# A feed-forward kernel's start: w1's first tile on ScalarE's queue, and the first contraction tile multiplied by halves of the rows

## The chip, the core and the metric

The kernel runs on one core of a Trainium2 chip. A core has a matrix engine (TensorE, PE in the profile; its weight loads are listed as PEld), a vector engine (VectorE, DVE), an activation engine (ScalarE, ACT), GpSimd (POOL) and SyncE (SP). Each has its own instruction stream; they meet through semaphores. Matrix products are written to PSUM, here 8 banks of 128 rows by 512 32-bit columns; everything else lies in SBUF, with 128 rows (partitions). SyncE and ScalarE start transfers between the device memory and SBUF, each on a queue of its own.

The metric is the device time of one execution in microseconds. Before the change its median over 3 runs is 126.36 us (126.25 to 126.38).

## What is computed

```python
B, S, D, F = 1, 2048, 640, 1728          # bf16
h = jnp.einsum("bsd,df->bsf", x, w1)     # x: (1, 2048, 640), w1: (640, 1728)
h = silu(h)                              # h * sigmoid(h)
out = jnp.einsum("bsf,fd->bsd", h, w2)   # w2: (1728, 640)
```

## The kernel before

**Tiling.** The contraction length D = 640 of the first product is cut into DT = 5 tiles of 128 ("contraction tiles", the index `dt`). F = 1728 is cut into 13 columns of 128 (`ft`) and a last one of 64. The 2048 rows of x are handled in four chunks of SCH = 512 rows (`sc`), and a chunk in four blocks of 128 rows (JB = 4). The first product is made transposed: PSUM gets h's 128 values of `ft` on its partitions and 512 rows of x along its columns, so w1's tile [128 x 128] is the loaded weight and the transposed x, `xT_sb[:, dt, rows]`, is streamed. One bank holds one (`ft`, `sc`). Sigmoid runs on ScalarE, and VectorE multiplies it with the sums (`silu`, L196); the result `hT_sb` is the weight or the streamed operand of the second product (L300 to L350), whose results go out by DMA.

**How x gets transposed.** For chunks 1 to 3, and for the last contraction tile of chunk 0, a transposing DMA brings x into `xT_sb` (L157, L237). For the first four contraction tiles of chunk 0, x is loaded as it lies into `x0_sb` (L143) and transposed by PE, 128 x 128 at a time, against an identity (`transpose_x0`, L171): four transposes write one PSUM bank, and one copy takes them from there to `xT_sb`, on VectorE for even `dt` (L180) and on ScalarE for odd `dt` (L182).

**The order of the work.** The program is a list of operations (`Plan`, L21); each goes to its engine's stream in the order in which it was added, with waits on the semaphores of what it depends on. An engine thus works strictly in the order written. PE's stream begins like this:

1. warm-up: five matmuls of 512 columns and one of 256 on constants, whose results are not used (L169);
2. the four transposes of contraction tile 0 of x, in two halves of two blocks each, with a bank and a VectorE copy for each half (L275);
3. more warm-up: one matmul of 512 columns and one of 256 (L277);
4. `column_group` for chunk 0 (L252): for each `dt`, one matmul of 512 columns into each of FA = 6 banks (`ft` 0 to 5). The first matmul of a `dt` waits for x's and w1's tile of that `dt`. After the second matmul (`ft == 1`) the transposes of the next `dt` are put in (`transpose_next`, L269);
5. `unit` for the other columns of chunk 0 (L211), then the other chunks, and then the second product.

**The loads at the start.** SyncE issues: the first half (two of four blocks) of x's tile 0 (`x0_a`, 64 KB), w1's tiles 0, 1 and 2 for the first six columns (192 KB each), then, after a wait for x's tile 0, w1's tiles 3 and 4; then the transposing DMA of x's tile 4 (after w1's tile 1 has landed) and the rest of w1 in two pieces. ScalarE issues: the second half of x's tile 0 (`x0_b`, 64 KB), x's tiles 1, 2 and 3 (128 KB each), and then loads its activation table. In the code (L151 to L154):

```python
x0_a = [load_x0("sp", "x0_a", 0, JB // 2, 0, 1), load_x0("act", "x0_b", JB // 2, JB, 0, 1)]
w1_lo = [load_w1("sp", "w1_0", 0, 1, 0, FA * P)]
x0_c = [load_x0("act", "x0_c", 0, JB, 1, 2), load_x0("act", "x0_d", 0, JB, 2, 3), ...]
w1_lo += [load_w1("sp", f"w1_{dt}", dt, dt + 1, 0, FA * P) for dt in (1, 2)]
```

The functions that the diff touches, with the profile's line numbers:

Of the kernel before, what the change touches and what calls it, by code (L numbers as in the profile page):

```python
# [20 lines left out]
class Plan:  # L21
# [9 lines left out]
    def add(self, eng, emit, deps=(), group=None):  # L31
        op = Op(eng, emit, [d for d in deps if d is not None], group)
        self.ops.append(op)
        return op
# [40 lines left out]
def bass_standalone__dense_activation_silu__prompt_kernel(  # L75
# [13 lines left out]
    P = 128  # L89
    H = P // 2  # L90
    SCH = 512
    DT = D // P
# [5 lines left out]
    JB = SCH // P  # L98
# [4 lines left out]
    with ExitStack() as es:  # L103
        def sb(name, shape, dtype):
            return es.enter_context(nc.sbuf_tensor(name, shape, dtype))

        xT_sb = sb("xT_sb", [P, DT, S], bf16)
        w1_sb = sb("w1_sb", [P, DT, F], bf16)
# [9 lines left out]
        ps = es.enter_context(nc.psum_tensor("ps", [P, NBANK, SCH], fp32))  # L118
# [6 lines left out]
        add = plan.add  # L125
        bank_free = [[] for _ in range(NBANK)]
        turn = [0]

        def take_bank():
            b = turn[0] % NBANK  # L130
            turn[0] += 1
            return b


        FA = 6
# [7 lines left out]
        def load_x0(eng, name, j0, j1, d0, d1):  # L143
            return add(eng, lambda e: e.dma_start(
                out=x0_sb[:, j0:j1, d0 * P:d1 * P], in_=x0_v[:, j0:j1, d0 * P:d1 * P]), group=name)

        def load_w1(eng, name, d0, d1, f0, f1, deps=()):
            return add(eng, lambda e: e.dma_start(
                out=w1_sb[:, d0:d1, f0:f1], in_=w1_v[:, d0:d1, f0:f1]), deps, group=name)

        x0_a = [load_x0("sp", "x0_a", 0, JB // 2, 0, 1), load_x0("act", "x0_b", JB // 2, JB, 0, 1)]  # L151
        w1_lo = [load_w1("sp", "w1_0", 0, 1, 0, FA * P)]
        x0_c = [load_x0("act", "x0_c", 0, JB, 1, 2), load_x0("act", "x0_d", 0, JB, 2, 3), load_x0("act", "x0_e", 0, JB, 3, 4)]
        w1_lo += [load_w1("sp", f"w1_{dt}", dt, dt + 1, 0, FA * P) for dt in (1, 2)]  # L154
        add("act", lambda e: e.activation(out=warm_sb[:, :], in_=warm_sb[:, :], func=ACT.Sigmoid), [warm])  # L155
# [1 line left out]
        x0_last = add("sp", lambda e: e.dma_start_transpose(  # L157
            out=xT_sb[:, DT - 1, 0:SCH], in_=xf[0:SCH, (DT - 1) * P:D]), w1_lo[1:2], group="x0_t")
# [5 lines left out]
        def warm_up(columns):  # L164
            for n in columns:
                add("pe", lambda e, n=n: e.matmul(  # L166
                    ps[:, NBANK - 1, 0:n], lhsT=ones[:, 0:P], rhs=ones[:, 0:n], start=True, stop=True))
# [3 lines left out]
        def transpose_x0(dt, j0, j1, b):  # L171

            dst = ps[:, b, :].bitcast(bf16)[:, j0 * P:j1 * P]
            out = xT_sb[:, dt, j0 * P:j1 * P]
            for j in range(j0, j1):
                t = add("pe", lambda e, j=j: e.transpose(  # L176
                    dst[:, (j - j0) * P:(j - j0 + 1) * P], x0_sb[:, j, dt * P:(dt + 1) * P], ident[:, :]),
                    [x0_a[j // (JB // 2)], id_b] if dt == 0 else [x0_c[min(dt, 3) - 1]] + bank_free[b])
            if dt % 2 == 0:
                c = add("dve", lambda e: e.tensor_copy(out=out, in_=dst), [t])  # L180
            else:
                c = add("act", lambda e: e.copy(out=out, in_=dst), [t])  # L182
            bank_free[b] = [c]
            return c

        def x_deps(sc, c0, n):
            return x0T if sc == 0 else x1_of if sc == 1 else [x_dma[sc]]

        def w1_deps(ft):
            return [w1_dma[max(g for g in range(len(w1_dma)) if w1_cuts[g] <= ft)]] if ft >= FA else w1_lo  # L190
# [5 lines left out]
        def silu(b, parts, n, pe):  # L196
            s = sig_turn[0] % NSIG
            sig_turn[0] += 1
            a = add("act", lambda e: e.activation(  # L199
                out=sig_sb[:, s, 0:n], in_=ps[:, b, 0:n], func=ACT.Sigmoid), [pe, sig_free[s]])  # L200
            for rows, ft, cols in parts:
                v = add("dve", lambda e, rows=rows, ft=ft, cols=cols: e.tensor_tensor(  # L202
                    out=hT_sb[rows, ft, cols], in0=ps[rows, b, 0:n], in1=sig_sb[rows, s, 0:n],
                    op=ALU.mult), [a])
                chunk_done[cols.start // SCH] = v
                if ft == FR:
                    tail_done[cols.start // SCH] = v
            bank_free[b] = [v]
            sig_free[s] = v

        def unit(sc, ft, c0, n):  # L211
            b = take_bank()
            cols = slice(sc * SCH + c0, sc * SCH + c0 + n)
            for dt in range(DT):
                pe = add("pe", lambda e, dt=dt: e.matmul(  # L215
                    ps[:, b, 0:n], lhsT=w1_sb[:, dt, ft * P:(ft + 1) * P], rhs=xT_sb[:, dt, cols],
                    start=(dt == 0), stop=(dt == DT - 1)),
                    x_deps(sc, c0, n) + w1_deps(ft) + bank_free[b] if dt == 0 else ())
            silu(b, [(slice(0, P), ft, cols)], n, pe)

        def tail_unit(sc):
            b = take_bank()
            for dt in range(DT):
                for hh in range(2):
                    pe = add("pe", lambda e, dt=dt, hh=hh: e.matmul(  # L225
                        ps[hh * H:(hh + 1) * H, b, :], lhsT=w1_sb[:, dt, FR * P:F],
                        rhs=xT_sb[:, dt, (sc + hh) * SCH:(sc + hh + 1) * SCH],
                        start=(dt == 0), stop=(dt == DT - 1), skip_group_check=True),
                        x_deps(sc, 0, SCH) + x_deps(sc + 1, 0, SCH) + w1_deps(FR) + bank_free[b]
                        if dt == 0 else ())  # L230
            silu(b, [(slice(hh * H, (hh + 1) * H), FR, slice((sc + hh) * SCH, (sc + hh + 1) * SCH))
                     for hh in range(2)], SCH, pe)

        x_dma, x1_of, w2_dma = {}, [], []
        for sc in range(1, NSC):
# [7 lines left out]
            if sc == 2:  # L243
                half = FR // 2
# [6 lines left out]

        def column_group(sc, x_dep, w1_dep, between=None):  # L252

            banks = [take_bank() for _ in range(FA)]
            for dt in range(DT):
                for ft in range(FA):
                    deps = bank_free[banks[ft]] if dt == 0 else []
                    if ft == 0:
                        deps = deps + [x_dep[dt], w1_dep[dt]]
                    pe = add("pe", lambda e, dt=dt, ft=ft: e.matmul(  # L260
                        ps[:, banks[ft], :], lhsT=w1_sb[:, dt, ft * P:(ft + 1) * P],
                        rhs=xT_sb[:, dt, sc * SCH:(sc + 1) * SCH],
                        start=(dt == 0), stop=(dt == DT - 1)), deps)
                    if dt == DT - 1:
                        silu(banks[ft], [(slice(0, P), ft, slice(sc * SCH, (sc + 1) * SCH))], SCH, pe)
                    if between and ft == 1:
                        between(dt + 1)

        def transpose_next(dt):  # L269
            if dt < DT - 1:  # L270
                x0T.append(transpose_x0(dt, 0, JB, FA + dt % 2))
            elif dt == DT - 1:
                x0T.append(x0_last)

        half = [transpose_x0(0, k * JB // 2, (k + 1) * JB // 2, FA - 2 + k) for k in range(2)]  # L275
        x0T = [half[1]]
        warm_up([SCH, 2 * P])  # L277
        column_group(0, x0T, w1_lo, transpose_next)
        for ft in range(FA, FR):
            unit(0, ft, 0, SCH)  # L280

        for sc in range(1, NSC):
            if sc == 1:
                column_group(sc, x1_of, w1_lo)
            for ft in range(FA if sc == 1 else 0, FR):
                unit(sc, ft, 0, SCH)
        reg_done = dict(chunk_done)
# [111 lines left out]
```

## Time and profile before

| | |
|---|---|
| median of 3 runs | 126.36 us (126.25 to 126.38) |
| the profiled execution's own time | 126.17 us |
| its span, first to last instruction of the program | 124.8 us |
| PE busy | 121.4 us (97% of the span) |
| weight loads (PEld) | 57.0 us (46%) |
| VectorE, ScalarE busy | 45.1 us (36%), 39.5 us (32%) |
| DMA | 10.41 MB, 83 GB/s over the span |
| warm-up matmuls (L166) | 8, 3.3 us |
| transposes on PE (L176) | 16, 263 ns each |
| matmuls of the two column groups (L260) | 387 ns each |
| ScalarE's copy of a transposed tile (L182) | 2, 586 ns each |

The times come from one profiled execution; its zero is the program's first instruction. A matmul's listed duration reaches from its start to the end of its results, and matmuls overlap in the array: what one costs PE is the distance from one start to the next, and not its listed duration. The page's clock row gives the granted clock of PE by slices. The waits name the engine whose semaphore came last.

### The profile page before, as it was taken

What the parts mean: (1) busy time and instruction counts of PE and PEld (TensorE: products, weight loads), DVE (VectorE), ACT (ScalarE), POOL (GpSimd) and SP (SyncE); (2) the same over time, 40 slices, a digit from 0 to 9 for tenths busy, and PEclk for the clock granted to TensorE, in tenths of its full rate; (3) what the DMA queues carried; (4) which work ended last, traced back from release to release, by engine and by line L of the source; (5) the groups of instructions that cost most, each with busy time, mean ns of one, the idle gap of its engine ahead of it and who ended that gap; (6) DMA issues with size and microseconds to landing.
All of it is one profiled execution on the core that took longest, in us unless ns stands there. A gap on an engine that the chain in (4) does not pass through costs nothing.

```text
span 124.8 us, 2088 instructions
## 1 busy us (share of the span) xinstructions
PE 121.4 (97%) x893; PEld 57.0 (46%) x898; DVE 45.1 (36%) x71; ACT 39.5 (32%) x69; POOL 0.7 (1%) x6
## 2 busy tenths in 40 slices
PE   7999999999999999999999999999999999999992
PEld 2454444444444444444444444444444444445481
DVE  0112984079666666666673020202021120202022
ACT  0614953097555555555530010101011010101021
POOL 2000000000000000000000000000000000000000
PEclk9999999999999999999999999999999999999999
DMA  3998474479940000000000001114120201112415
GB/s 70 325 230 307 106 96 84 94 202 385 305 90 0 0 5 0 3 0 0 0 0 5 0 0 32 26 21 174 47 105 5 105 0 21 26 21 74 158 67 149
DMA packets 20169, 10.41 MB, mean 83 GB/s; under 512 B 14400, under 2 KB 20160, under 8 KB 20160
## 3 DMA queue, kind: packets, MB, share of 16 engines
q1 hardware_dynamic: 18016, 9.69, 28.1%
q10 hardware_dynamic: 2144, 0.59, 2.0%
q8 instruction: 7, 0.11, 0.4%
q14 instruction: 2, 0.02, 0.0%
HBM read 5.03 MB, written 2.62 MB: 61 GB/s over the span
## 4 chain that ended last, share of the span: by engine, by line
PE 97%; DVE 0%; issue 0%
PE ps L323 47%; PE ps L215 34%; PE ps L260 11%; PE ps L166 3%; PE ps L225 2%; PE ps L176 1%; DVE o_sb L334 0%
## 5 line engine op out<-in xcount | busy, mean ns | idle before, releaser
L323 PE MATMUL ps<-w_sb,hT_sb 64*128 64x512 bf16 (+2 forms) x486 | 47.3, 352 | 0.0
L202 DVE TENSOR_TENSOR hT_sb<-ps,sig_sb 128x512 bf16<-128x512 f32 (+1 forms) x56 | 37.0, 688 | 21.8 <-ACT sig_sb L199 21.7
L215 PE MATMUL ps<-xT_sb,w_sb 128*128 128x512 bf16 x197 | 43.3, 379 | 0.2
L199 ACT ACTIVATE sig_sb<-ps 128x512 bf16<-128x512 f32 x54 | 30.7, 605 | 24.6 <-PE ps L215 16.4
L323 PEld LDWEIGHTS ps<-w_sb,hT_sb 64*128 64x128 bf16 x486 | 23.3, 94 | 23.7
L215 PEld LDWEIGHTS ps<-xT_sb,w_sb 128*128 128x128 bf16 x200 | 19.6, 98 | 23.6
L334 DVE CAST o_sb<-ps 128x512 bf16<-128x512 f32 (+2 forms) x9 | 5.7, 633 | 37.6 <-PE ps L323 37.6
L336 ACT CAST o_sb<-ps 128x512 bf16<-128x512 f32 (+2 forms) x9 | 4.8, 539 | 38.6 <-PE ps L323 38.6
L260 PE MATMUL ps<-xT_sb,w_sb 128*128 128x512 bf16 x58 | 14.1, 387 | 0.1
L323 PE MATMUL ps<-hT_sb,w_sb 64*128 64x512 bf16 x108 | 12.3, 376 | 0.0
L260 PEld LDWEIGHTS ps<-xT_sb,w_sb 128*128 128x128 bf16 x60 | 5.6, 99 | 6.8 <-ACT xT_sb L182 0.6
L323 PEld LDWEIGHTS ps<-hT_sb,w_sb 64*128 64x128 bf16 x108 | 5.2, 94 | 6.6 <-issue 0.4
L334 DVE CAST oT_sb<-ps 128x512 bf16<-128x512 f32 x2 | 1.4, 692 | 11.7 <-PE ps L323 11.7
L336 ACT CAST oT_sb<-ps 128x512 bf16<-128x512 f32 x2 | 1.2, 586 | 13.6 <-PE ps L323 13.6
L166 PE MATMUL ps<-const-bfloat16-1.0 128*128 128x512 bf16 (+1 forms) x8 | 3.3, 571 | 0.8 <-PEq L384 0.8
L180 DVE COPY xT_sb<-ps 128x256 bf16<-128x256 bf16 (+1 forms) x3 | 0.9, 336 | 5.8 <-PE ps L176 5.8
L225 PE MATMUL ps<-xT_sb,w_sb 128*64 128x512 bf16 x20 | 2.3, 381 | 0.0
L182 ACT COPY xT_sb<-ps 128x512 bf16<-128x512 bf16 x2 | 1.2, 586 | 3.7 <-PE ps L176 3.7
L155 ACT ACT_TABLE_LOAD x1 | 1.3, 1283 | 2.9 <-issue 2.9
L176 PEld LDWEIGHTS ps<-ident,x_sb 128*128 128x128 bf16 x16 | 1.5, 114 | 1.5 <-DMA x_sb<-in_x_dram 0.7
L176 PE MATMUL ps<-ident,x_sb 128*128 128x128 bf16 x16 | 2.0, 263 | 0.0
L166 PEld LDWEIGHTS ps<-const-bfloat16-1.0 128*128 128x128 bf16 x8 | 1.0, 136 | 1.9 <-issue 1.9
(9 smaller groups left out, 2.3 us busy)
## 6 DMA issues: line engine op xcount, KB each, us to landing
out_dram<-o_sb SPq DMA_DIRECT2D x14, 160.0 KB, 1.9
w_sb<-in_w_dram SPq DMA_DIRECT2D x1, 1120.0 KB, 7.6
w_sb<-in_w_dram SPq DMA_DIRECT2D x5, 192.0 KB, 3.7
w_sb<-in_w_dram SPq DMA_DIRECT2D x1, 960.0 KB, 5.2
w_sb<-in_w_dram SPq DMA_DIRECT2D x1, 640.0 KB, 4.6
w_sb<-in_w_dram SPq DMA_DIRECT2D x1, 560.0 KB, 5.4
x_sb<-in_x_dram ACTq DMA_DIRECT2D x3, 128.0 KB, 3.7
xT_sb<-in_x_dram SPq DMA_TRANSPOSE x16, 3.6
```

Of the source, the lines that this page charges most:

```text
L155: add("act", lambda e: e.activation(out=warm_sb[:, :], in_=warm_sb[:, :], func=ACT.Sigmoid), [warm])
L166: add("pe", lambda e, n=n: e.matmul(ps[:, NBANK - 1, 0:n], lhsT=ones[:, 0:P], rhs=ones[:, 0:n], start=True, stop=True))
L176: t = add("pe", lambda e, j=j: e.transpose(dst[:, (j - j0) * P:(j - j0 + 1) * P], x0_sb[:, j, dt * P:(dt + 1) * P], ident[:, :]), [x0_a[j ...
L182: c = add("act", lambda e: e.copy(out=out, in_=dst), [t])
L199: a = add("act", lambda e: e.activation(out=sig_sb[:, s, 0:n], in_=ps[:, b, 0:n], func=ACT.Sigmoid), [pe, sig_free[s]])
L202: v = add("dve", lambda e, rows=rows, ft=ft, cols=cols: e.tensor_tensor(out=hT_sb[rows, ft, cols], in0=ps[rows, b, 0:n], in1=sig_sb[rows, ...
L215: pe = add("pe", lambda e, dt=dt: e.matmul(ps[:, b, 0:n], lhsT=w1_sb[:, dt, ft * P:(ft + 1) * P], rhs=xT_sb[:, dt, cols], start=(dt == 0), ...
L225: pe = add("pe", lambda e, dt=dt, hh=hh: e.matmul(ps[hh * H:(hh + 1) * H, b, :], lhsT=w1_sb[:, dt, FR * P:F], rhs=xT_sb[:, dt, (sc + hh) * ...
L260: pe = add("pe", lambda e, dt=dt, ft=ft: e.matmul(ps[:, banks[ft], :], lhsT=w1_sb[:, dt, ft * P:(ft + 1) * P], rhs=xT_sb[:, dt, sc * SCH:( ...
L323: pe = add("pe", lambda e, b=b, n=n, lhsT=lhsT, rhs=rhs, ft=ft: e.matmul(ps[:, b, 0:n], lhsT=lhsT, rhs=rhs, start=(swap == 0 and ft == 0), ...
L334: ev = add("dve", lambda e, b=b, n=n, dst=dst: e.tensor_copy(out=dst, in_=ps[:, b, 0:n]), [pe])
L336: ev = add("act", lambda e, b=b, n=n, dst=dst: e.copy(out=dst, in_=ps[:, b, 0:n]), [pe])
```

## The change

- w1's tile 0 is no longer SyncE's second transfer but ScalarE's first. x's second half of tile 0, until now ScalarE's first transfer, becomes SyncE's second.
- Of the warm-up after the first transposes, the matmul of 256 columns is left out.
- For `dt` = 0 the column group goes over the six columns twice, first with the first 256 rows of x and then with the other 256, each time with matmuls of 256 columns into one half of the bank. Other `dt` are done with 512 columns as before. In chunk 1 every `dt` has one part.
- Only the first half's two transposes stand ahead of the column group. Those of the second half come after the third matmul of the first pass; they and their copy now use bank 7 (FA + 1), the first half's bank 6.
- The transposes of contraction tile 1 come after the sixth matmul of the first pass, ahead of the whole second pass; they too use bank 7, and wait for the copy of the second half. Those of tiles 2 and 3 stay after the second matmul of the `dt` before.

```diff
-        x0_a = [load_x0("sp", "x0_a", 0, JB // 2, 0, 1), load_x0("act", "x0_b", JB // 2, JB, 0, 1)]
-        w1_lo = [load_w1("sp", "w1_0", 0, 1, 0, FA * P)]
+        x0_a = [load_x0("sp", "x0_a", 0, JB // 2, 0, 1)]
+        w1_lo = [load_w1("act", "w1_0", 0, 1, 0, FA * P)]
+        x0_a.append(load_x0("sp", "x0_b", JB // 2, JB, 0, 1))
...
-            return x0T if sc == 0 else x1_of if sc == 1 else [x_dma[sc]]
+            return x0T[-1] if sc == 0 else x1_of if sc == 1 else [x_dma[sc]]
...
             for dt in range(DT):
-                for ft in range(FA):
-                    deps = bank_free[banks[ft]] if dt == 0 else []
-                    if ft == 0:
-                        deps = deps + [x_dep[dt], w1_dep[dt]]
-                    pe = add("pe", lambda e, dt=dt, ft=ft: e.matmul(
-                        ps[:, banks[ft], :], lhsT=w1_sb[:, dt, ft * P:(ft + 1) * P],
-                        rhs=xT_sb[:, dt, sc * SCH:(sc + 1) * SCH],
-                        start=(dt == 0), stop=(dt == DT - 1)), deps)
...
-                    if between and ft == 1:
-                        between(dt + 1)
-
-        def transpose_next(dt):
-            if dt < DT - 1:
-                x0T.append(transpose_x0(dt, 0, JB, FA + dt % 2))
-            elif dt == DT - 1:
-                x0T.append(x0_last)
-
-        half = [transpose_x0(0, k * JB // 2, (k + 1) * JB // 2, FA - 2 + k) for k in range(2)]
-        x0T = [half[1]]
-        warm_up([SCH, 2 * P])
+                parts = len(x_dep[dt])
+                for h in range(parts):
+                    c0, c1 = h * (SCH // parts), (h + 1) * (SCH // parts)
+                    for ft in range(FA):
+                        deps = [x_dep[dt][h], w1_dep[dt]] if ft == 0 else []
+                        if dt == 0 and h == 0:
+                            deps = deps + bank_free[banks[ft]]
+                        pe = add("pe", lambda e, dt=dt, ft=ft, h=h, c0=c0, c1=c1: e.matmul(
+                            ps[:, banks[ft], c0:c1], lhsT=w1_sb[:, dt, ft * P:(ft + 1) * P],
+                            rhs=xT_sb[:, dt, sc * SCH + c0:sc * SCH + c1],
+                            start=(dt == 0 and h == 0), stop=(dt == DT - 1), skip_group_check=True), deps)
...
+                        if between:
+                            between(dt, h, ft)
+
+        x0T = [[transpose_x0(0, 0, JB // 2, FA), None]]
+
+        def transpose_next(dt, h, ft):
+            if (dt, h, ft) == (0, 0, 2):
+                x0T[0][1] = transpose_x0(0, JB // 2, JB, FA + 1)
+            elif (dt, h, ft) == (0, 0, FA - 1) or dt in range(1, DT - 2) and ft == 1:
+                x0T.append([transpose_x0(dt + 1, 0, JB, FA + (dt + 1) % 2)])
+            elif (dt, ft) == (DT - 2, 1):
+                x0T.append([x0_last])
+
+        warm_up([SCH])
         column_group(0, x0T, w1_lo, transpose_next)
...
-                column_group(sc, x1_of, w1_lo)
+                column_group(sc, [[d] for d in x1_of], w1_lo)
```

More of the change, by code (lines that the diff above doesn't have):

```diff
@@ L255, in column_group @@
             for dt in range(DT):
-                for ft in range(FA):
-                    deps = bank_free[banks[ft]] if dt == 0 else []
-                    if ft == 0:
-                        deps = deps + [x_dep[dt], w1_dep[dt]]
-                    pe = add("pe", lambda e, dt=dt, ft=ft: e.matmul(
-                        ps[:, banks[ft], :], lhsT=w1_sb[:, dt, ft * P:(ft + 1) * P],
-                        rhs=xT_sb[:, dt, sc * SCH:(sc + 1) * SCH],
-                        start=(dt == 0), stop=(dt == DT - 1)), deps)
-                    if dt == DT - 1:
-                        silu(banks[ft], [(slice(0, P), ft, slice(sc * SCH, (sc + 1) * SCH))], SCH, pe)
-                    if between and ft == 1:
-                        between(dt + 1)
@@ L269, in transpose_next @@
-        def transpose_next(dt):
-            if dt < DT - 1:
-                x0T.append(transpose_x0(dt, 0, JB, FA + dt % 2))
-            elif dt == DT - 1:
-                x0T.append(x0_last)
-        half = [transpose_x0(0, k * JB // 2, (k + 1) * JB // 2, FA - 2 + k) for k in range(2)]
-        x0T = [half[1]]
-        warm_up([SCH, 2 * P])
+                parts = len(x_dep[dt])
[9 more added lines that the diff above has]
+                            start=(dt == 0 and h == 0), stop=(dt == DT - 1), skip_group_check=True), deps)
+                        if dt == DT - 1:
+                            silu(banks[ft], [(slice(0, P), ft, slice(sc * SCH, (sc + 1) * SCH))], SCH, pe)
+                        if between:
+                            between(dt, h, ft)
```

## The prediction

> **What bounds the kernel now.** I read the page's busy shares and its chain first:
>
> ```profile
> span 124.8 us, 2088 instructions
> PE 121.4 (97%) x893; PEld 57.0 (46%) x898; DVE 45.1 (36%) x71; ACT 39.5 (32%) x69; POOL 0.7 (1%) x6
> PE 97%; DVE 0%; issue 0%
> ```
>
> TensorE (PE) is the chain. I then looked for gaps in its matmul starts: from the first real matmul (4.21 us) to the last at 122.24, there is none over 0.1 us: every step is one matmul long (single steps of exactly two, every 10.8 us, are missing records). So whatever moves PE at the start moves the end as much. The timeline of the start (start, length, engine, line; in brackets the idle time before, and what ended it):
>
> ```profile
> 0.77 2.50 PE L166 MATMUL ps<-const-bfloat16-1.0 128*128 128x512 bf16 x6 [0.77 <-PEq L384]
> 3.07 0.63 PE L176 MATMUL ps<-ident,x_sb 128*128 128x128 bf16 x4
> 3.50 0.84 PE L166 MATMUL ps<-const-bfloat16-1.0 128*128 128x512 bf16 x2
> 3.53 0.51 DVE L180 COPY xT_sb<-ps 128x256 bf16<-128x256 bf16 x2 [2.63 <-PE ps L176]
> 4.18 0.14 PEld L260 LDWEIGHTS ps<-xT_sb,w_sb 128*128 128x128 bf16 x2 [0.53 <-DVE xT_sb L180]
> 4.21 1.01 PE L260 MATMUL ps<-xT_sb,w_sb 128*128 128x512 bf16 x2
> 5.02 0.61 PE L176 MATMUL ps<-ident,x_sb 128*128 128x128 bf16 x4
> 5.45 1.48 PE L260 MATMUL ps<-xT_sb,w_sb 128*128 128x512 bf16 x6
> 5.66 0.59 ACT L182 COPY xT_sb<-ps 128x512 bf16<-128x512 bf16 x1 [1.23 <-PE ps L176]
> 6.30 0.13 PEld L260 LDWEIGHTS ps<-xT_sb,w_sb 128*128 128x128 bf16 x2 [0.30 <-ACT xT_sb L182]
> 6.76 0.39 PE L176 MATMUL ps<-ident,x_sb 128*128 128x128 bf16 x4
> 6.98 1.46 PE L260 MATMUL ps<-xT_sb,w_sb 128*128 128x512 bf16 x6
> 8.28 0.39 PE L176 MATMUL ps<-ident,x_sb 128*128 128x128 bf16 x4
> ```
>
> Steps from one group's start to the next give prices. Four transposes take 0.43 us at 5.02 (107 ns each) but 0.22 at 6.76 (56); the six matmuls from 6.98 to 8.28 take 1.30 (216 each), while the single starts of the pair at 4.21 lie 381 and 427 apart. The clock thus doubles near 5.47; the clock column says 1.00 throughout and doesn't show it. So any PE time saved before 5.47 is worth half of itself. A 512-column and a 256-column matmul fill 3.50 to 4.14: 0.427 and 0.213, linear in columns. Warm, a line through 56 (128 columns) and 216 (512) gives 109 ns for 256.
>
> Landings, from the trace's semaphore updates: x's tile 0, first half 2.96, second 3.24; w1's tile 0 4.08; x's tile 1 4.59; w1's tile 1 5.08; x's tile 2 5.52. So it was w1's tile 0 that PE waited for at 4.21 (4.08, and 0.13 to start), by 0.07 us after its warm-up. The row at 6.30 shows the other thing to keep in mind: tile 1's first weight load starts the moment ACT's copy is done, and its matmul (6.33) just keeps the cadence.
>
> **The change part by part.**
>
> *Loads.* The slots stay: SP still issues three ahead of its first wait and ACT four, at 0.33 to 0.57 us each, so ACT's table load still comes near 2.91 and the next x tiles' issues (1.26, 1.79, 2.35) keep their times to 0.1. POOL issues nothing; the identity is ready before 1.5. w1's tile 0 is issued at 0.74 in place of 1.25, x's second half at 1.25 in place of 0.74. SP now waits for that half before w1's tiles 3 and 4: it may hold them from 3.32 to about 4, but their data queued until 6.99 and 7.50 anyway, and PE reads them after 9: no cost. w1's tile 0 took 2.83 from issue to landing, which from 0.74 gives 3.56; bounds: 2.94 (a 64 KB half's 2.2) and 4.08 (no gain). I take 3.56, its own row; up to 3.80 nothing changes, as follows. The second half of x lands between 3.24 and about 4.1 (changed places with w1's tile 0) and is wanted at 4.49. x's tile 1 has the same bytes ahead of it as before, 320 KB: 4.59, wanted at 5.35.
>
> *Warm-up.* The 256-column matmul after the transposes goes, with 0.213 us, and two of four transposes leave the stretch ahead of real work (0.213).
>
> *First real matmul.* The first half's two transposes still start at 3.07 (behind warm-up, and behind the landing at 2.96). The first DVE copy runs 3.53 to 3.82, as before; from a copy's end to the next matmul the 6.25 → 6.33 pair shows 0.078: start 3.90. The remaining warm-up ends at 3.71, so 0.19 idle, under the full warm-up of before at no cost. Gain 0.31 us at half clock, worth 0.155.
>
> *Tile 0 in halves.* Matmuls go from 6 x 512 columns to 12 x 256. Cold: three halves (0.167, the first being 46 ns short as at 4.21, then 0.213 twice) to 4.49; two transposes to 4.71; three halves to 5.35; then tile 1's four transposes. These reuse the bank of the second half, so they wait for its DVE copy: last transpose starts 4.60, plus 0.31, 0.04 and 0.29 as in the 3.39 → 3.82 rows: 5.24, read at 5.29, 0.06 before it would cost. With the clock at 5.47 the four start at 5.35, 5.45, 5.52, 5.58 and end at 5.63. The second six halves need 6 x 109 = 0.654: to 6.29.
>
> *The wait that appears.* Tile 1 cannot start before ACT has copied it: last transpose's start 5.58, +0.22 its length, +0.04, +0.586 copy, +0.078: 6.49. Before, four full matmuls (0.864) lay between these transposes and the reader, and the copy's path from the transposes' end is 0.863: exactly covered (the row at 6.30). Now six halves, 0.654, cover it: PE is idle 0.21 us, warm, at full price. Queued behind is all of PE's program; ACT and DVE wait for PE anyhow. From there the code is that of before (transposes of tiles 2 and 3 after two matmuls), so no second wait.
>
> *Sum.* Tile 1's first matmul: 6.33 → 6.49, +0.17. By parts, in warm time: -0.155 (earlier start), +0.112 (two transposes now inside), +0.01 (12 x 109 against 6 x 216), +0.21 (wait), rounding aside. Nothing absorbs it: w1's next piece landed at 10.94 and is read at 11.95. The profiled execution's own time is 126.17 us (span 124.8 and 1.4 around it), 0.19 under the median: 126.34 on its basis, **126.5** against the median of 126.36.
>
> The doubling at 5.47 is kept as it stands in that one trace.
>
> **Rivals.** All are compared at tile 1's first matmul, 6.33 before.
>
> *Slower: x's first half is held up by w1's tile 0.* They are issued 3 ns apart on two queues. On each of 16 DMA engines the half is 16 packets of 17 ns (239 packets, 42.6% in 1.8 to 2.4) and w1's tile 8 of 66 ns (0.53 us; between 6.2 and 6.6, with w1's packets alone in flight, some 104 of them took 107% of 16 engines). If the tile gets in between, the half lands up to 0.53 later; transposes, copy and matmul follow 1:1, to 4.43 at most, worth 0.27: 126.80. w1's tile landing as late as 4.08 gives 4.21 and half of 0.31: 126.69. For: each engine was near full from 2.2 on. Against: landings of x and w1 tiles alternate cleanly later (4.59, 5.08, 5.52), whole transfers in turn, and SP's data came first by 0.27. It decides from a start of 4.07 on, where the sum passes +0.25. [...]
>
> *Not slower: the wait doesn't appear.* If the clock switches after 7 us in both programs, six cold halves (1.28) cover the copy (0.88), and 0.31 earlier less two transposes' 0.21 leaves -0.10: 126.3. The same if the copy path is 0.2 shorter than its row: -0.04. Against: 586 ns is the same in both ACT copies.
>
> *Faster: the clock switches much earlier in the new program*, at 4.0: PE warm from 3.90, 12 x 109 + 6 x 56 + two waits of 0.21 put tile 1 at 5.96: 126.0. For: 5.47 is the row of one execution. Against: its warm-up to 3.07 is unchanged.
>
> *Slower: the clock switches later in the new program*, whose PE idles 0.19 us before 3.90. By 0.5 us: tile 1's transposes go cold and end at 5.83, the last one's copy is done at 6.64, and its matmul starts at 6.71: +0.39, 126.75. By a second stretch as long as the 4.7 us from PE's start to the switch, it would cost up to 2.3. For: the switch has one row. Against: PE stays 94% busy from 2.06 to 5.47, real matmuls fill more of that than before, and the four times shown lie within 0.21 us, so the switch hardly moved between them. [...]
>
> **How the numbers follow.** My sum 0.50; held-up loads 0.22 (the bytes' order speaks for it, the alternation against); no wait 0.15; early clock 0.07; late clock 0.06. A measurement can tell about 0.2% (0.25 us) from no change. The sum's own range, 126.4 to 126.7, crosses that bound with a sixth of its chance. Same: 0.42 + 0.15; slower: 0.08 + 0.22 + 0.06; faster 0.07. The range 126.2 to 126.85 holds the sum, the absent wait and the held-up loads, and leaves out the two clocks.
>
> **What would show it.** Right: w1's tile 0 landing before 3.8; the first matmul of 256 columns on w1 at 3.9; a 0.2 us PE gap before tile 1's matmuls ended by ACT's copy, near 6.3 to 6.5; clock doubling at 5.5; PE without gaps afterwards and its last matmul 0.17 later. Wrong: a first matmul after 4.05, transposes waiting for x, a switch more than 0.3 from 5.47, or no gap before tile 1.

## The result

The changed kernel takes 126.80 us (median of 14 runs, 126.33 to 127.17) beside 126.22 us for the kernel before on the same chip (14 runs, 125.43 to 126.38): a ratio of 1.0048, 95% interval 1.0032 to 1.0063, so 0.40 to 0.80 us slower. Measured once more on another occasion (the run e9 below) the ratio was 1.0034 (1.0019 to 1.0048). The forecast was 126.5 against 126.36 us (+0.17 us at tile 1's first matmul); the time is in the stated range, at the place of the rival in which x's first half is held up. Ratios leave out runs over 1.5% above the fastest of their kernel (two of e2's 8, two of e4's 12, two of e7's 11), medians don't.

The page of the changed kernel, its span, busy shares and chain by engine and by line:

```profile
span 125.4 us, 2104 instructions
PE 122.0 (97%) x903; PEld 57.3 (46%) x903; DVE 45.2 (36%) x71; ACT 39.4 (31%) x69; POOL 0.7 (1%) x6
PE 95%; DMA 2%; DVE 0%; issue 0%
PE ps L331 47%; PE ps L216 34%; PE ps L266 11%; DMA x_sb<-in_x_dram 2%; PE ps L226 2%; PE ps L177 1%; PE ps L167 0%; DVE o_sb L342 0%
```

PE's share of the chain was 97% and is 95%: the other 2% are a load of x, which wasn't in the chain before. The chain in order of time (start, length, what), its first pieces, shows where it sits:

```profile
0.67 0.06 issue
0.73 2.88 DMA x_sb<-in_x_dram
3.61 0.05 issue
3.65 0.39 PE ps L177 x2
4.05 0.43 PE ps L167
4.47 0.78 PE ps L266 x3
```

The chain now starts with the transfer of x's first half, 2.88 us long, in place of PE's warm-up. The timeline of the start, as shown for the kernel before, some rows left out (L177 are the transposes, L266 the matmuls on w1, L183 and L181 the copies, L167 the warm-up):

```profile
3.65 0.39 PE L177 MATMUL ps<-ident,x_sb 128*128 128x128 bf16 x2 [0.37 <-DMA x_sb<-in_x_dram]
3.84 0.63 PE L167 MATMUL ps<-const-bfloat16-1.0 128*128 128x512 bf16 x1
4.09 0.29 DVE L181 COPY xT_sb<-ps 128x256 bf16<-128x256 bf16 x1 [3.19 <-PE ps L177]
4.43 0.82 PE L266 MATMUL ps<-xT_sb,w_sb 128*128 128x256 bf16 x3
5.05 0.42 PE L177 MATMUL ps<-ident,x_sb 128*128 128x128 bf16 x2
5.26 0.84 PE L266 MATMUL ps<-xT_sb,w_sb 128*128 128x256 bf16 x3
5.94 0.38 PE L177 MATMUL ps<-ident,x_sb 128*128 128x128 bf16 x4
6.16 1.45 PE L266 MATMUL ps<-xT_sb,w_sb 128*128 128x256 bf16 x8
6.36 0.58 ACT L183 COPY xT_sb<-ps 128x512 bf16<-128x512 bf16 x1 [2.00 <-PE ps L177]
7.00 0.11 PEld L266 LDWEIGHTS ps<-xT_sb,w_sb 128*128 128x128 bf16 x2 [0.30 <-ACT xT_sb L183]
```

The first transposes start at 3.65 (3.07 before), with PE idle for a load. Real work, the first matmul on w1, starts at 4.43 (4.21 before, 3.90 forecast). Tile 1's first weight load follows ACT's copy at 7.00; single matmul starts in the trace are 6.709 for the last half matmul and 7.004 for tile 1, where the cadence would have put it at 6.82: 0.19 us of waiting. Tile 1 starts 0.68 us later than before (6.33), and PE's last matmul starts 0.69 later (122.24 and 122.93): nothing is given back in between.

Why x's first half comes late shows in the DMA queues. For 1.8 to 2.4 us, the kernel before (q1 is SyncE's queue, q10 ScalarE's; packets, MB, share of 16 engines):

```profile
q1 hardware_dynamic: 239, 0.06, 42.6%
q10 hardware_dynamic: 111, 0.03, 20.4%
```

and the changed kernel in the same stretch:

```profile
q10 hardware_dynamic: 38, 0.06, 59.8%
q1 hardware_dynamic: 10, 0.00, 1.7%
```

Of the 256 data packets of x's first half some 230 had started by 2.4 us before the change (the 239 count the transfers' semaphore writes too), and 10 after it. In their place 38 of w1's 128 packets went, and slowly: the five that started first took 308 ns each on the average, the next twenty 157, most of the later ones 65. SyncE had started x's half at 0.732, ScalarE w1's tile at 0.747, but issuing the latter took 0.43 us and the former 0.45: the issue of w1's tile ended first, by 11 ns. x's half landed at 3.61 (2.96 before), w1's tile 0 at 3.44.

### The profile page after: what moved, and what is told of

It is laid out like the page before. It is cut to its first block, busy times and chain, and to the rows that moved or that the text cites. A ratio compares the mean times of both kernels' runs of the same rounds, so it can differ in the third digit from the quotient of the medians.

```text
span 125.4 us, 2104 instructions
## 1 busy us (share of the span) xinstructions
PE 122.0 (97%) x903; PEld 57.3 (46%) x903; DVE 45.2 (36%) x71; ACT 39.4 (31%) x69; POOL 0.7 (1%) x6
## 4 chain that ended last, share of the span: by engine, by line
PE 95%; DMA 2%; DVE 0%; issue 0%
PE ps L331 47%; PE ps L216 34%; PE ps L266 11%; DMA x_sb<-in_x_dram 2%; PE ps L226 2%; PE ps L177 1%; PE ps L167 0%; DVE o_sb L342 0%
## 5 line engine op out<-in xcount | busy, mean ns | idle before, releaser
L216 PE MATMUL ps<-xT_sb,w_sb 128*128 128x512 bf16 x200 | 43.5, 379 | 0.0
L216 PEld LDWEIGHTS ps<-xT_sb,w_sb 128*128 128x128 bf16 x200 | 19.6, 98 | 23.6
L266 PE MATMUL ps<-xT_sb,w_sb 128*128 128x512 bf16 (+1 forms) x66 | 14.8, 373 | 0.0
L266 PEld LDWEIGHTS ps<-xT_sb,w_sb 128*128 128x128 bf16 x66 | 6.3, 101 | 6.7 <-ACT xT_sb L183 0.6
L167 PE MATMUL ps<-const-bfloat16-1.0 128*128 128x512 bf16 (+1 forms) x7 | 3.1, 597 | 0.8 <-PEq L392 0.8
L181 DVE COPY xT_sb<-ps 128x256 bf16<-128x256 bf16 (+1 forms) x3 | 1.0, 336 | 6.4 <-PE ps L177 6.4
L183 ACT COPY xT_sb<-ps 128x512 bf16<-128x512 bf16 x2 | 1.2, 585 | 4.4 <-PE ps L177 4.4
L177 PE MATMUL ps<-ident,x_sb 128*128 128x128 bf16 x16 | 2.0, 241 | 0.4 <-DMA x_sb<-in_x_dram 0.4
L177 PEld LDWEIGHTS ps<-ident,x_sb 128*128 128x128 bf16 x16 | 1.3, 106 | 1.9 <-DMA x_sb<-in_x_dram 1.1
L167 PEld LDWEIGHTS ps<-const-bfloat16-1.0 128*128 128x128 bf16 x7 | 0.9, 138 | 1.8 <-issue 1.8
```

The source lines that it names most:

```text
L167: add("pe", lambda e, n=n: e.matmul(ps[:, NBANK - 1, 0:n], lhsT=ones[:, 0:P], rhs=ones[:, 0:n], start=True, stop=True))
L177: t = add("pe", lambda e, j=j: e.transpose(dst[:, (j - j0) * P:(j - j0 + 1) * P], x0_sb[:, j, dt * P:(dt + 1) * P], ident[:, :]), [x0_a[j ...
L216: pe = add("pe", lambda e, dt=dt: e.matmul(ps[:, b, 0:n], lhsT=w1_sb[:, dt, ft * P:(ft + 1) * P], rhs=xT_sb[:, dt, cols], start=(dt == 0), ...
L266: pe = add("pe", lambda e, dt=dt, ft=ft, h=h, c0=c0, c1=c1: e.matmul(ps[:, banks[ft], c0:c1], lhsT=w1_sb[:, dt, ft * P:(ft + 1) * P], rhs= ...
```

## The experiments

Two causes were held against each other: the loads, and PE's new order with its wait; then what decides about the loads; then the clock. Times of a run are compared with the kernel before, run beside it on the same chip. "Switch" is the time at which PE's clock doubles, read from the trace's clock record, or from the steps between matmuls in the six profiles without one.

### e1: PE's new order, the loads of before

```diff
-        x0_a = [load_x0("sp", "x0_a", 0, JB // 2, 0, 1)]
-        w1_lo = [load_w1("act", "w1_0", 0, 1, 0, FA * P)]
-        x0_a.append(load_x0("sp", "x0_b", JB // 2, JB, 0, 1))
+        x0_a = [load_x0("sp", "x0_a", 0, JB // 2, 0, 1), load_x0("act", "x0_b", JB // 2, JB, 0, 1)]
+        w1_lo = [load_w1("sp", "w1_0", 0, 1, 0, FA * P)]
```

> PE's order is that of the changed kernel, the loads are those of before. Theory A (two causes: the loads delay x's first half, and PE's new order adds a wait for ScalarE's copy of tile 1): x's first half lands near 2.96 us, w1's tile 0 near 4.08, PE starts real work at 4.21 as before; then 0.11 us for two transposes that now lie inside, 0.01 for smaller matmuls and 0.2 for the wait, so +0.33 us at an equal clock switch, about 126.55; PE idle 0.2 us before tile 1's matmuls. Rival (all of the loss comes from the loads and the later clock switch): no idle time before tile 1's matmuls, the time of before within 0.1%.

Measured: 126.46 against 126.13 us, ratio 1.0019 (0.9999 to 1.0038), that is -0.01 to +0.48 us. x's first half landed at 2.92, w1's tile 0 at 4.18, transposes at 3.07; real work started at 4.31, 0.10 later than before, because w1's tile landed 0.10 later. The wait is there: the last half matmul starts at 6.568, tile 1's first at 6.863, 0.186 late, and its weight load follows ACT's copy:

```profile
6.22 0.58 ACT L182 COPY xT_sb<-ps 128x512 bf16<-128x512 bf16 x1 [1.79 <-PE ps L176]
6.86 0.11 PEld L265 LDWEIGHTS ps<-xT_sb,w_sb 128*128 128x128 bf16 x2 [0.30 <-ACT xT_sb L182]
```

The wait belongs to PE's order and not to the loads; the time agrees with 0.33 but doesn't exclude zero.

### e2: the new loads, PE's order of before

The same edit the other way round, in the kernel before.

> The loads are those of the changed kernel, PE's order is that of before. Theory A: x's first half again lands near 3.6 us and the second near 4.3, behind w1's tile 0 (3.4); both halves' transposes now stand ahead of real work, so the second half is transposed from 4.38, the warm-up of 0.64 us follows, and the first real matmul starts near 5.2, 1.0 us later than before: +0.5 us at an equal clock switch, about 126.7. Rival (the loss is PE's order, the loads' change is harmless or the late landing was of one execution): x's first half lands before 3.1, the time of before within 0.1%.

Measured: 127.5 against 126.13 us, ratio 1.0082 (1.0052 to 1.0111), so 0.66 to 1.40 us slower. x's first half landed at 3.56, its second at 4.30, w1's tile 0 at 3.39; real work started at 5.18. So the new loads cost by themselves, and the late half is no accident of one execution. The forecast for the time (+0.5) was too small. In the profiled execution (128.54 us, the second longest of the 8) the clock still stood at half rate at 9.0 us, which half a microsecond doesn't cover; how much of the median comes from that, no run here shows.

### e3: w1's tile 0 started 0.2 us later

```diff
-        w1_lo = [load_w1("act", "w1_0", 0, 1, 0, FA * P)]
+        w1_lo = [load_w1("act", "w1_0", 0, 1, 0, FA * P, [warm])]
```

> The changed kernel, but ScalarE starts w1's tile 0 only after VectorE's first memset, some 0.2 us later. Theory A (which of the two first transfers is served first is settled by which is issued first, and w1's tile won by some 15 ns): x's first half lands near 2.96 us, w1's tile 0 at 3.5 to 3.8, real work starts near 3.9, PE then waits 0.2 us for the copy of tile 1: +0.17 us against the kernel before at an equal clock switch. Rival (the two transfers share the engines, whichever comes first): x's first half still lands after 3.25, real work starts after 4.1.

Measured: 126.45 against 126.13 us, ratio 1.0012 (0.9997 to 1.0026). w1's tile was issued at 0.93 in place of 0.75. x's half landed at 3.28, real work started at 4.11: the rival's figures, by 0.03 and 0.01 us, though not its mechanism on every engine. The 16 engines' arrivals of x's half lie in two groups: four engines at 2.40 to 2.49, twelve at 2.88 to 3.28. The queues from 1.8 to 2.4 us:

```profile
q1 hardware_dynamic: 122, 0.03, 21.8%
q10 hardware_dynamic: 17, 0.03, 13.2%
```

Of the 122 packets 118 are x's (four are the semaphore writes of the four early engines). They had all started by 2.17; the next one started at 2.48. At 16 packets an engine, 64 of the 118 belong to the four early engines, so 54 to the other twelve. There x's half did not stand behind the whole of w1's tile: part of it went ahead, then its packets paused for 0.3 us, while w1's began. In this pause the engines were busy for 24% only, with 16 packets of w1; what else held x's packets is not shown. So 0.2 us of lead lets the whole of x's half through first on four engines alone: what counts is not only which is issued first.

### e5: the two first transfers exchanged between the queues

```diff
-        x0_a = [load_x0("sp", "x0_a", 0, JB // 2, 0, 1)]
-        w1_lo = [load_w1("act", "w1_0", 0, 1, 0, FA * P)]
+        x0_a = [load_x0("act", "x0_a", 0, JB // 2, 0, 1)]
+        w1_lo = [load_w1("sp", "w1_0", 0, 1, 0, FA * P)]
```

> The changed kernel with the first two transfers exchanged between the queues: x's first half on ScalarE's, w1's tile 0 on SyncE's. Theory A (w1's tile is handed over sooner whatever the queue, since its issue takes 0.43 us against 0.45 to 0.49 for the half of x, and its slow first packets then stand ahead of x on each engine): x's first half again lands near 3.6 us, PE's first transposes start after 3.5. Rival (ScalarE's queue was favoured): x's first half lands before 3.1, PE's first transposes at 3.07.

Measured (one execution, 126.85 us): x's half landed at 3.59, w1's tile at 3.37. The queues from 1.8 to 2.4 us:

```profile
q1 hardware_dynamic: 47, 0.07, 77.9%
```

and PE's first transposes:

```profile
3.63 0.39 PE L177 MATMUL ps<-ident,x_sb 128*128 128x128 bf16 x2 [0.36 <-DMA x_sb<-in_x_dram]
```

No packet of x moved before 2.4 us, now on ScalarE's queue. It isn't the queue: w1's tile went first from either, when the two were issued together (here its issue ended 0.08 us ahead of that of x's half).

### e7: w1's tile 0 started 0.75 us later

```diff
+        w1_lo = [load_w1("act", "w1_0", 0, 1, 0, FA * P, [id_b])]
```

> The changed kernel, but ScalarE starts w1's tile 0 only after GpSimd has finished the identity, at 1.5 us in place of 0.75. Theory A (x's first half is late only because w1's packets stand ahead of it on the engines): the half lands on all engines before 2.75, w1's tile 0 near 4.1, real work starts at 4.2 to 4.3, and the sum is the 0.33 us of PE's new order against the kernel before at an equal clock switch. Rival (SyncE's first transfer is late for another reason, such as the second half behind it on the same queue): it lands after 3.0.

Measured: 126.9 against 125.73 us, ratio 1.0074 (1.0045 to 1.0103). x's half landed on all engines at 2.39 to 2.66, earlier than in any other run:

```profile
q1 hardware_dynamic: 281, 0.07, 49.8%
```

(the queues from 1.8 to 2.4 us: all of x's first half and the start of its second, nothing of w1). The transposes start at 3.07 again. So it is w1's load that holds x up, and the second half behind it on SyncE's queue is not. The delay went over to that second half, which w1's tile now followed by 0.24 us: it landed at 4.40 (3.24 in the kernel before). The price was misjudged: w1's tile landed at 4.83, not at 4.1, 3.35 us after its issue where it took 2.83 in the kernel before, and real work started at 4.97:

```profile
4.97 0.80 PE L266 MATMUL ps<-xT_sb,w_sb 128*128 128x256 bf16 x3 [1.05 <-DMA w_sb<-in_w_dram]
```

### e6 and e11: tile 1's copy on VectorE

```diff
-            if dt % 2 == 0:
+            if dt in (0, 1, 3):
                 c = add("dve", lambda e: e.tensor_copy(out=out, in_=dst), [t])
```

> The changed kernel with tile 1's copy on VectorE in place of ScalarE, and tile 2's on ScalarE (tile 0 and 3: VectorE). Theory A (the idle time before tile 1's matmuls is the copy's length beyond what six half matmuls cover): the copy takes 0.42 us in place of 0.59, the idle time of 0.19 us falls to 0.02 to 0.04, 0.16 us less at an equal clock switch, about 126.65 where the changed kernel had 126.8. Rival (another thing ends this wait, w1's tile 1 which landed at 6.07): the idle time stays at 0.15 or more.

> The changed kernel with tile 1's copy on VectorE, for another look, since in the first one the clock doubled at 7.1 us and hid any wait. Theory A, if the clock doubles before 6.2 this time: PE's idle time before tile 1's matmuls is 0.02 to 0.05 us in place of 0.19. Rival: 0.15 or more.

In e6 the switch came at 7.10, the half matmuls took 213 ns each and hid any copy: inconclusive on the wait (126.79 against 125.73 us, ratio 1.0078, 1.0053 to 1.0102; the changed kernel itself was not run beside it). This is the rival of the prediction in which the wait doesn't appear; e7, with the copy still on ScalarE and the switch at 8.51, shows it too (the last half matmul at 7.907, tile 1's first at 8.120, one full step later). In e11 the switch came at 6.07:

```profile
6.22 1.29 PE L266 MATMUL ps<-xT_sb,w_sb 128*128 128x256 bf16 x8
6.42 0.42 DVE L181 COPY xT_sb<-ps 128x512 bf16<-128x512 bf16 x1 [0.61 <-PE ps L177]
```

The copy takes 0.42 us in place of 0.58. Tile 1's first matmul starts at 6.906, the last half matmul at 6.768, so PE waits 0.03 us in place of 0.19. In that execution w1's tile 1 landed at 6.43, well before. The wait is the copy's length beyond its cover.

### e4: the kernel before without the middle warm-up

```diff
-        warm_up([SCH, 2 * P])
```

> The kernel before without the two warm-up matmuls between the first transposes and real work: PE idles from 3.5 to 4.2 us, nothing else moves. Theory A (idle time ahead of the switch delays the clock's doubling): the switch comes later than in the kernel before, by 0.5 us or more on the average of the runs, and the time is 0.25 us or more longer. [...]

Measured: 126.07 against 126.13 us, ratio 0.9983 (0.9960 to 1.0005). PE idled from 3.50 to 4.09, and the switch came at 4.54, earlier than 5.47. Ten of the 12 runs took 125.49 to 126.73, and their interval excludes theory A's 0.25 us for them. The other two took 128.36 and 128.41, where none of the 31 of the kernel before took more than 126.64; no profile shows what they did, and the spread is wider than that of the kernel before. So idle time didn't delay the switch as a rule; whether it did in those two stays open.

### e8: the kernel before once more

> The kernel before, once more, for the time of the clock's doubling alone. Theory A (the switch has a phase of its own in each execution): it comes more than 0.1 us from 5.47, with PE's order and its landings as before, and the profiled time differs from 126.17 by half the distance. Rival (the program sets it): 5.47 again to 0.1 us.

Measured: 125.91 us, switch near 3.85 (the warm-up matmul at 3.50 is still followed after 0.39 us, the matmul at 4.28 after 0.215). So the switch isn't set by the program: the prediction took its one row for a fixed quantity. But the time fell by 0.26 us (on another chip), and the start of PE's last matmul by 0.13 (122.24, 122.11), not by half of 1.6. Real work began 0.07 later, and then a load ended a wait of PE:

```profile
4.28 0.59 PE L260 MATMUL ps<-xT_sb,w_sb 128*128 128x512 bf16 x2
5.10 0.40 PE L176 MATMUL ps<-ident,x_sb 128*128 128x128 bf16 x4 [0.22 <-DMA x_sb<-in_x_dram]
```

x's tile 1 landed at 5.05, and its transposes, due at 4.71, started at 5.10, 0.39 late. With this early clock the kernel before waits for its loads.

### e9, e10, e12: the changed kernel again, with its idle time filled, and with VectorE's copy too

```diff
-        warm_up([SCH] * 5 + [2 * P])
+        warm_up([SCH] * 5 + [2 * P, SCH, P])
...
-        warm_up([SCH])
+        warm_up([SCH, P])
```

> The changed kernel once more, beside the next one on the same chip. [...]

> The changed kernel with PE's two idle stretches ahead of real work filled by warm-up: one matmul of 512 and one of 128 columns before the first transposes, one of 128 after them. [...] Rival (idle time doesn't matter): the median of the changed kernel to 0.1 us.

> Both mends together: PE's idle stretches filled, and tile 1's copy on VectorE. [...] Rival (the wait was not the copy's length): no gain over the filled kernel.

Measured, on one chip beside 126.36 us for the kernel before: e9 126.78 (ratio 1.0034, 1.0019 to 1.0048), e10 126.86 (1.0037, 1.0016 to 1.0058), e12 126.79 (1.0034, 1.0017 to 1.0050). Filling the idle time brought nothing that shows: e10's median is 0.08 us above e9's, as its rival had it. e9's own size, 0.42 us, is near 0.44, the 0.11 for the later start and the 0.33 for PE's order, and its interval (0.24 to 0.61) holds the first measurement (0.58) too. Both mends together brought nothing either that an interval of 0.3 us can show.

e9 happened to be profiled with the switch at 3.82, and shows what an early clock meets in the changed kernel. From its chain in order of time, the pieces around the waits:

```profile
0.73 2.68 DMA x_sb<-in_x_dram
4.24 0.50 PE ps L266 x3
4.74 0.13 PE ps L177 x2
4.89 0.30 DVE xT_sb L181
5.33 0.38 PE ps L177 x4
6.39 0.60 PE ps L266 x2
7.03 0.40 PE ps L177 x4
```

Three waits stand in it, by single matmul starts: tile 1's transposes at 5.33 are due at 5.02 and wait 0.31 for the second half's copy, whose bank they reuse; tile 1's matmuls wait 0.19 for ACT's copy; tile 2's transposes at 7.03 are due at 6.83 and wait 0.20 for x's tile 2, landed at 6.98. In e12, where the switch was early too, the first of these is 0.31 again, the second 0.08 and the third 0.31; the second is now ended by w1's tile 1 (landed at 6.311, matmul at 6.446, the same 0.135 as from 4.076 to 4.211 in the kernel before), no longer by the copy. Two executions with an early clock, e8 and e9, differ by 0.44 us at PE's last matmul (122.11 and 122.55).

## Why the prediction was wrong where it was

The range held, the sum behind it didn't: its first term had the wrong sign, its wait was right. That the time is in the range is owed to the rival of held-up loads, which the range was drawn to include.

*Loads: the step that failed.* "The first half's two transposes still start at 3.07 ... behind the landing at 2.96" assumed that x's half keeps its place on the engines. It landed at 3.61 (3.41 to 3.72 in the seven other profiles that start the two together), and real work started at 4.43 in place of 3.90, the rival's "4.43 at most". That this figure was met is luck in part: the half landed 0.64 us later, more than the 0.53 of the rival, and the transposes followed the landing after 0.05 us, where they had stood 0.11 behind it before. The argument against that rival, that whole transfers take turns and SyncE's data came first by 0.27, is half true: in the changed kernel the transfers do go one after the other, but for a few packets (the 16 arrivals of x's half, in order, come 0.16 to 0.20 us after those of w1's tile), but w1's tile is the first of them. w1's tile 0 (3.56 forecast, 3.44) and x's tile 1 (4.59, 4.16) were right or better.

Why w1's tile goes first stays open. That the 11 ns between the ends of the two issues decide is only argued, and e3 speaks against it as the whole rule: there the issue of x's half ended 0.12 us ahead (1.20, 1.32), and twelve engines were late all the same. That the half can be split shows in e3, where 54 of the 192 packets of the twelve late engines went ahead; how many an engine took at a time can't be read there, nor what made the pause of 0.3 us. The rival's time, 126.80, is the measured median, but by chance to the digit: it stood for +0.44 us, and +0.58 was measured against a kernel before that was 0.14 us faster than in the forecast.

*The wait for ACT's copy: right.* 0.21 forecast, 0.19 in the changed kernel and in e1, 0.03 with the shorter copy. The steps were right too: 213 ns and 109 ns for 256 columns.

*The bank's second use: a step too small.* The copy was to end 0.11 us before the transposes were due and to be read 0.05 after its end, with 0.06 to spare. In the changed kernel it ended at 5.80, 0.10 before they were due, but they started 0.145 after its end, as in all ten profiles with this order (0.145 to 0.147): 0.04 late, and 0.31 late where the clock was early.

*The switch: wrong.* It was kept at 5.47 because four times lay within 0.21 us. The profiled executions show 3.85 and 5.47 for the kernel before, 3.82 and 5.96 for the changed one, 7.10 in e6, 8.51 in e7 and 9.4 in e2. The conclusion that "the switch hardly moved between them" drew too much from four runs; 14 of them spread over 0.95 us. That PE's busy share ahead of the switch, 94% from 2.06 to 5.47, bears on it was the author's estimate and is not shown: measured, PE was busy for 89% of this stretch in the changed kernel (3.04 us) and for all of it in the kernel before, and e10, with PE's idle time filled, was not faster.

*The sum.* At tile 1, +0.68 in the profile: 0.22 later start at half price, 0.11; two transposes inside, 0.11; smaller matmuls, 0.01; the bank's 0.04 at half price, 0.02; the wait, 0.19; the switch 0.48 later at half price, 0.24. The last term is this execution's own switch. Without it 0.44 us remain, near e9's difference of medians (0.42) and inside both intervals. That e8 against e9 gives 0.44 too is chance, for with their early clock other waits make it up (0.39 us in e8, 0.31, 0.19 and 0.20 in e9). The sum as put on record had -0.155 where +0.11 stands: the mis-sized term is the start of real work, 0.27 us.

*Slips that change nothing here.* SyncE issues four transfers ahead of its first wait, not three (0.73, 1.25, 1.75 and 2.22 us in the kernel before). x's second half landed at 4.34, later than its bound of 4.1, but was wanted only at 5.05 by then. In the rival of the later clock, four cold transposes from 5.35 end at 5.78 and not at 5.83, which takes some 0.03 us off it.

*Later loads: not foreseen.* In the changed kernel w1's tile 1 landed at 6.07 and x's tile 2 at 6.90, against 5.08 and 5.52 before; "the same bytes ahead" was checked for x's tile 1 alone. In the stretches view (from:to, length, busy times by engine, clock, DMA share, GB/s) the changed kernel has

```profile
3.90:5.10 1.20, 1.20 (x7) 0.48 (x5) 0.29 (x1) 0.45 (x2) 0.00 (x0) 1.00 0.65 174
```

where the kernel before has

```profile
3.90:5.10 1.20, 1.20 (x5) 0.33 (x4) 0.13 (x1) 0.52 (x2) 0.00 (x0) 1.00 1.13 317
```

The engines stand a third idle there although w1's tile 1 and x's tile 2 had been issued at 1.77 and 1.72. Every profile with w1's tile 0 at the head of a queue has x's tile 2 at 6.75 or later, e1, e4 and e8 with the old loads at 5.6 to 6.2. Why the engines idle stays open. It costs nothing with a switch near 6 us, where tile 2 is wanted at 7.45, and 0.2 to 0.3 us with an early one (0.18 in e3, 0.20 in e9, 0.31 in e12).

What stays open besides: no version was found that is faster than the kernel before; and how much of each median is owed to the mean time of the switch was not separated.

## What to carry to other kernels

Two transfers that are started together on two queues need not share evenly: from 1.8 to 2.4 us 38 packets of w1's tile went and 10 of x's half. Here the packets that moved first said more than the order of issue, and the smaller transfer, for which the first instruction waits, needed a real lead (0.2 us in e3 was too little, 0.75 in e7 enough). When a consumer is moved closer to its producer, compare what lies between them with the whole path through the copy before moving it: four full matmuls (0.864 us) just covered it, six halves (0.654) did not. And the time at which the clock doubled differed between executions, from 3.82 to 9.4 us here: take its spread from many runs before counting anything that lies ahead of it.

## What the runs showed of the hardware

- Some of w1's first packets are slow: of the 128 that started first, 10 to 19 took more than 150 ns in 13 of the 14 profiles, where most took 65 (in the changed kernel 10, the longest 575). In e3 none did, and x's half was late on twelve engines there too, so slow packets are not needed for the delay.
- The clock record gives the full-rate stretch as 119.466 us in seven executions of six different programs, and 122.880 us in e9. The two differ by 3.414 us; what sets the length, no run here tested.
- The switch came between 3.8 and 6.1 us in eleven of the 14 profiles, at 7.10 in e6, 8.51 in e7 and 9.4 in e2. Between two executions of one program it differed by 1.62 us in the kernel before (3.85, 5.47) and by 2.14 us in the changed kernel (3.82, 5.96); what sets it is not shown.
